# First expert's w2 in a row, guess's sums ahead of Newton's first step, two engines for the last stores, new step tables

## The chip, the cores and the metric

One core of a Trainium2 chip runs the whole kernel in one launch. The metric is device time in microseconds (us), from the first to the last work of the execution. Five engines take part, each working through a queue of its own in order: TensorE (PE, matmuls; PEld is its weight load), VectorE (DVE), ScalarE (ACT), GpSimd (POOL) and SyncE (SP, which issues most transfers).

## The reference

Nystrom attention over 8 batches x 8 heads, 576 tokens, head size 64, feeds a mixture of 8 experts (512 -> 1024 -> 512) in which a token either takes the expert of its own largest logit or keeps that of the token before.

```python
q_lm, k_lm = q.reshape(B,H,32,18,D).mean(3), k.reshape(B,H,32,18,D).mean(3)
A, Bm, C = sm(q, k_lm), sm(q_lm, k_lm), sm(q_lm, k)     # softmax of scaled products
Z = Bm.T / (norm1(Bm) * norminf(Bm) + 1e-6)
for _ in range(6): Z = 2 * Z - Z @ Bm @ Z               # Newton
x = A @ Z @ C @ v                                       # then [b, s, H * D]
logits = x @ w_gate
e = argmax(logits[b, s]) if s == 0 or sigmoid(x @ w_local) < 0.5 else prev_e
out[b, s] = softmax(logits)[e] * (relu(x[b, s] @ w1[e]) @ w2[e])
```

## The kernel before, in words

**Work.** For each batch the kernel computes A (32 landmarks by 576 tokens per head) and a small matrix W = Z C v, folds W into the expert's first weights (G = W w1, `w_w1`), and runs one expert over the batch's 576 tokens (`expert`): the expert that most of the batch's tokens take. Tokens of other experts are gathered later in slots of 128 (`slot_tokens` and so on; the sequence is batches 0 to 6, one slot, batch 7). Products that need full precision split an operand in a high and a low part, h and l: `split_w2` makes wh with a cast on ACT (line 720) and wl with a subtraction on POOL (line 725); `w_w1` makes gh on ACT (line 707) and gl on DVE (line 708).

**The expert.** A batch takes 16 chunks (`CH`): eight hidden tiles f for tokens 256 to 575 (first pass), then eight for tokens 0 to 255 (second pass). In a chunk `mm1` does six matmuls (line 737) into a PSUM bank, ACT and DVE make h, and two chunks later the second product (line 789, for a 64-token rest line 781) adds to the output banks. `store` scales the result and writes it out. The last stores of the kernel are those of blocks 0 and 1 of batch 7.

**Order.** All steps of the attention of the next batches are interleaved with the chunks by tables of times in chunks: `FIRST` (rest of batch 0), `SECOND` (batch 1), `PLANS` (batches 2 to 7), `W2_AT` (in which chunk of batch 0 the w2 tiles of batch 1 are loaded), `G_AT` (in which two chunks G of the next batch is made), `SLOT_AT`. A step with time t is emitted ahead of the half chunk that begins next. Up to the ninth chunk (`IN_ROW`) the PE's instructions are tied to the order of emission; the prologue ties PE, ACT, DVE and POOL. What is not tied, all of SP's issues among it, is ordered by the framework's scheduler by its own simulated times.

**The prologue** (`first_attention`, line 1009 on) works off batch 0 with nothing to overlap. There the first expert is guessed from the column sums of v: `guess_sums` (line 539, five matmuls for each of four head pairs, on PE), `guess_copy` (line 545, ACT), `guess_scores` (lines 551 and 554, PE and ACT), `guess` (lines 559 and 560, DVE). The index goes to a register of SP, and `first_weights` (line 1215) issues w1 in two pieces and one half, and w2 tiles of 256 KB each, four of which fit in the buffers `raw2` (`load_w2`, line 715; w1 by line 671). `keep_warm` (line 176) are matmuls without a use of their own. Newton's steps are line 432, the product C v is line 345. After the prologue `cuts_at` emits the split of tile 4 + i in chunk i.

**Gates of a batch.** `gates` (line 570) makes logits, `votes` (`eq`, line 584, then a matmul, line 588, and the index, line 593) picks the batch's expert, `get_w1` loads its weights. The room of v is one buffer (`v_t`, line 224): v of the next batch can only be loaded when C v of this one is done.

Of the kernel before, what the change touches and what calls it, by code (L numbers as in the profile page):

```python
# [9 lines left out]
F32 = mybir.dt.float32  # L10
# [10 lines left out]
P = 128  # L21
# [55 lines left out]
def nystrom_attn_then_sticky_moe(ctx, tc, qT, kT, v, wg, w12, out):  # L77
# [93 lines left out]
    def keep_warm(n, pz=None):  # L171


        pz = one.tile([P, 512]) if pz is None else pz
        for _ in range(n):
            nc.tensor.matmul(pz, zeros[:, 0:P], zeros[:, 0:pz.shape[1]], start=True, stop=True)
# [623 lines left out]
    def store(b, st, k, yp):  # L800
        ys = fk.tile([P, DM], F32, name="ys", bufs=2)
        t0 = b * S + k * P
        if b == B - 1 and k == 1:

            nc.scalar.mul(out=ys[:, 0:256], in_=yp[:, 0:256], mul=st["pw"][:, k:k + 1])
            nc.vector.tensor_scalar(out=ys[:, 256:512], in0=yp[:, 256:512], scalar1=st["pw"][:, k:k + 1], scalar2=None, op0=ALU.mult)
            nc.scalar.dma_start(out=out[t0:t0 + P, 0:256], in_=ys[:, 0:256])
            nc.sync.dma_start(out=out[t0:t0 + P, 256:512], in_=ys[:, 256:512])
        elif k < 4:
            nc.scalar.mul(out=ys, in_=yp, mul=st["pw"][:, k:k + 1])  # L810
            nc.scalar.dma_start(out=out[t0:t0 + P, :], in_=ys)
# [196 lines left out]
    def first_attention(st, st1):  # L1008
# [294 lines left out]
    PLANS = {
        2: (-13.4, -10.9, -9.4, -12.4, -7.9, -8.9, -7.9, -6.9, -5.9, -5.4, -5.9, -4.4, -1.9, -5.4, -1.9, -2.4, -0.9,
            -0.4, -0.9, -0.4, -0.4, 0.1, 2.1, -0.4, 3.6, 4.1, 5.1, 5.6, 6.6, 7.1, 8.1, 10.1, 8.1, 8.1, 8.6, 13.6,
            14.1),
        3: (-22.4, -16.9, -21.9, -15.9, None, -15.4, -13.4, -13.4, -13.4, -9.9, -8.9, -8.4, -6.4, -7.4, -2.9, -7.9,
            -8.4, -5.4, -6.9, -3.9, -2.9, -4.4, -3.9, -2.9, 1.1, 2.6, 2.6, 2.6, 3.1, 4.6, 3.6, 5.1, 8.1, 4.1, 7.6,
            10.1, 10.1),
        4: (-23.4, -17.9, -20.4, -16.9, None, -18.4, -15.9, -15.9, -15.4, -15.9, -14.4, -13.4, -11.4, -11.9, -10.4,  # L1310
            -9.4, -7.4, -7.4, -5.9, -8.4, -5.9, -6.4, -5.4, -7.4, -4.9, -5.4, -3.4, -2.9, 2.6, 3.1, 2.6, 3.1, 4.1,
            4.1, 4.1, 6.6, 10.1),
        5: (-26.4, -17.9, -24.4, -22.9, None, -16.9, -17.4, -16.9, -15.9, -16.4, -12.9, -14.9, -10.9, -11.4, -9.4,
            -11.9, -10.9, -10.4, -8.4, -10.4, -9.4, -9.4, -6.9, -3.9, -4.4, -1.9, -0.9, 1.6, 1.6, 2.1, 2.6, 4.6, 4.1,
            4.1, 4.1, 4.1, 6.1),
        6: (-21.9, -17.9, -20.9, -20.9, None, -17.4, -17.9, -16.9, -14.4, -14.4, -13.9, -13.9, -10.9, -12.4, -9.9,
            -12.4, -9.9, -9.9, -5.9, -8.4, -6.9, -8.9, -4.9, -4.9, -0.9, -3.4, -3.4, -2.4, 1.1, 2.1, 1.6, 4.6, 3.6,
            4.6, 4.6, 7.1, 7.6),
        7: (-26.9, -20.4, -25.4, -19.9, None, -20.9, -21.4, -17.9, -15.4, -15.9, -14.9, -13.9, -13.4, -14.4, -11.4,
            -12.9, -11.4, -11.4, -11.9, -10.4, -9.9, -10.9, -10.9, -7.9, -4.9, -7.4, -4.9, -4.9, -0.4, -4.4, -0.4,  # L1320
            1.1, 2.6, 3.1, 7.6, 7.6, 10.6),
    }
    G_AT = {0: (14, 15), 1: (14, 15), 2: (12, 15), 3: (14, 15), 4: (11, 14), 5: (13, 15), 6: (11, 15), 7: (2, 7)}
    SLOT_AT = (-11.5, -7.5, -7.0, -4.0, -3.5, 0.5, 1.0, 8.0, 7.6, -1.0, 25.0)
# [115 lines left out]
```

## Time and profile before

| | us |
|---|---|
| median of 3 runs | 483.35 (483.09 to 485.33) |
| the profiled execution | 482.71 |
| its span, first to last instruction | 480.9 |
| PE busy in the span | 457.2 (95%), 4709 matmuls |
| DVE, POOL, ACT busy | 275.3, 233.5, 205.0 |
| SP's queue of transfers | 66.83 MB, 39.9% of 16 DMA engines |

PE is busy nearly all the time, so what can be had lies in its idle stretches. Such a table is an average: which engine or transfer ends a wait is read stretch by stretch, from the views further down.

### The profile page before, as it was taken

Reading aid. Unit: us, or ns where it says so; the run is one execution under the profiler, and the core shown is the slowest. Engines: PE = TensorE matmul, PEld = TensorE weight load, DVE = VectorE, ACT = ScalarE, POOL = GpSimd, SP = SyncE. Lnnn points to the kernel's source line nnn. Section 1 sums busy time; section 2 is a strip of 40 time slices with the busy share of each in tenths; the row PEclk is TensorE's granted clock in tenths of the full one; section 3 lists DMA queues with packets and bytes.
Section 4 is the critical chain, followed back from the end, with each engine's and each line's share of the span. In section 5 each row is a group of like instructions: output and inputs, shape, how many; then the busy total and the mean of one; then the engine's idle time right before and its main releaser. Section 6 shows DMA issues by size and latency. Waiting matters only on the chain.

```text
span 480.9 us, 12154 instructions
## 1 busy us (share of the span) xinstructions
PE 457.2 (95%) x4709; PEld 338.7 (70%) x4709; DVE 275.3 (57%) x823; ACT 205.0 (43%) x519; POOL 233.5 (49%) x365
## 2 busy tenths in 40 slices
PE   8977799989999999999999999999999999999995
PEld 3544567567776687667886688767886787778884
DVE  6886876676578447837832584337647845333121
ACT  2445344463354724436342733346332614455131
POOL 7276655189057525654922463244335755277010
PEclk9989999999999999999999999999999999999998
DMA  8797055694069505965842316521621802672011
GB/s 299 260 373 268 0 210 198 235 355 153 8 215 397 183 7 198 350 206 201 290 137 93 133 48 266 176 72 51 258 106 46 315 7 52 211 262 82 0 57 46
DMA packets 38861, 82.01 MB, mean 171 GB/s; under 512 B 3291, under 2 KB 4827, under 8 KB 38032
## 3 DMA queue, kind: packets, MB, share of 16 engines
q1 hardware_dynamic: 32064, 66.83, 39.9%
q10 hardware_dynamic: 5248, 9.31, 5.5%
q0 software_dynamic: 1488, 5.07, 2.8%
q8 instruction: 38, 0.62, 0.5%
q14 instruction: 23, 0.19, 0.1%
HBM read 66.29 MB, written 14.94 MB: 169 GB/s over the span
## 4 chain that ended last, share of the span: by engine, by line
PE 71%; DMA 8%; DVE 8%; issue 5%; ACT 5%; POOL 2%; SPq 1%; ACTq 0%; POOLq 0%; DVEq 0%
PE py L789 32%; PE ph L737 19%; PE pg L781 6%; DMA raw<-w 5%; PE one L345 2%; PE one L432 2%; PE ph L694 2%; PE one L304 2%; DMA out<-ys 1%; PE one L331 1%; PE one L482 1%; DMA q_t<-qT 1%; POOL wl L725 1%; ACT ys L810 1%; DVE eq L584 1%
## 5 line engine op out<-in xcount | busy, mean ns | idle before, releaser
L789 PE MATMUL py<-wh,h 128*128 128x512 f32 x528 | 170.9, 402 | 1.7 <-DVE h L749 1.0
L725 POOL TENSOR_TENSOR wl<-raw,wh 128x512 fp32r<-128x512 f32 x72 | 92.2, 1296 | 75.1 <-ACT wh L720 55.4
L789 PEld LDWEIGHTS py<-wh,h 128*128 128x128 f32 x528 | 95.4, 188 | 29.5 <-issue 5.9
L746 ACT ACTIVATE h<-ph 128x256 fp32r<-128x256 f32 (+2 forms) x136 | 54.7, 403 | 129.5 <-PE ph L737 104.9
L749 DVE SCALAR_TENSOR_TENSOR h<-ph,h 128x256 fp32r<-128x256 f32 (+1 forms) x136 | 55.7, 410 | 89.7 <-ACT h L746 85.6
L789 PE MATMUL py<-wl,h 128*128 128x512 f32 x264 | 91.7, 394 | 0.0
L737 PE MATMUL ph<-ath,gh 128*128 128x320 f32 (+1 forms) x256 | 80.1, 313 | 1.7 <-DVE gl L708 1.7
L737 PE MATMUL ph<-ath,gl 128*128 128x320 f32 (+1 forms) x256 | 76.1, 297 | 0.0
L737 PE MATMUL ph<-atl,gh 128*128 128x320 f32 (+1 forms) x256 | 75.9, 296 | 0.0
L737 PEld LDWEIGHTS ph<-ath,gh 128*128 128x128 f32 x256 | 48.4, 189 | 15.4 <-issue 6.4
L789 PEld LDWEIGHTS py<-wl,h 128*128 128x128 f32 x264 | 49.4, 188 | 10.5 <-issue 0.8
L737 PEld LDWEIGHTS ph<-atl,gh 128*128 128x128 f32 x256 | 48.4, 189 | 3.7
L737 PEld LDWEIGHTS ph<-ath,gl 128*128 128x128 f32 x256 | 48.3, 189 | 1.0 <-issue 0.8
L720 ACT CAST wh<-raw 128x512 fp32r<-128x512 f32 x72 | 43.1, 629 | 12.7 <-DMA raw<-w 10.3
L810 ACT ACTIVATE ys<-py,pall 128x512 f32<-128x512 f32 x31 | 20.7, 691 | 12.4 <-PE py L789 5.1
L819 POOL TENSOR_TENSOR ys<-ys,yl 64x512 f32<-64x512 f32 x8 | 10.2, 1277 | 32.3 <-ACT yl L817 32.3
L494 POOL TENSOR_TENSOR sa<-sa,mxa 128x1152 f32<-128x1152 f32 x7 | 14.9, 2133 | 22.5 <-DVE mxa L493 22.5
L708 DVE TENSOR_TENSOR gl<-ph,gh 128x512 fp32r<-128x512 f32 (+1 forms) x19 | 12.4, 658 | 22.1 <-ACT gh L707 22.0
L707 ACT CAST gh<-ph 128x512 fp32r<-128x512 f32 (+1 forms) x19 | 10.6, 562 | 28.7 <-PE pg L694 26.8
L241 POOL TENSOR_TENSOR t<-q_t 128x288 f32<-128x288 f32 x28 | 20.4, 746 | 4.7 <-DMA q_t<-qT 1.7
L781 PE MATMUL pg<-wl,h 128*128 128x512 f32 x56 | 22.4, 400 | 0.0
L781 PE MATMUL pg<-wh,h 128*128 128x512 f32 x56 | 22.0, 394 | 0.0
(335 smaller groups left out, 730.8 us busy)
## 6 DMA issues: line engine op xcount, KB each, us to landing
raw<-w SPq DMA_DIRECT2D x72, 256.0 KB, 5.8
raw<-w SPq DMA_DIRECT2D x17, 1024.0 KB, 7.0
v_t<-v SPq DMA_DIRECT2D x8, 1024.0 KB, 8.0
out<-ys ACTq DMA_DIRECT2D x31, 256.0 KB, 3.0
q_t<-qT SPq DMA_DIRECT2D x6, 1152.0 KB, 5.4
k_t<-kT SPq DMA_DIRECT2D x6, 1152.0 KB, 9.2
ad<-sa POOLq DMA_DIRECT2D x8, 576.0 KB, 3.1
q_t<-qT SPq DMA_DIRECT2D x4, 576.0 KB, 7.8
```

Of the source, the lines that this page charges most:

```text
L241: nc.gpsimd.tensor_add(t9[:, i], src[:, a + i, :, 0:9], src[:, a + i, :, 9:18])
L494: nc.gpsimd.tensor_tensor(out=sa, in0=sa, in1=mx.unsqueeze(2).broadcast_to([P, 2 * NJ, M]), op=ALU.subtract)
L707: st["cut"] = nc.scalar.copy(out=gh[:, g, x], in_=ps[g][:, 0:n * P]).ins.name
L708: last = nc.vector.tensor_tensor(out=gl[:, g, x], in0=ps[g][:, 0:n * P], in1=gh[:, g, x].bitcast(F32), op=ALU.subtract)
L720: cut = nc.scalar.copy(out=wh, in_=raw)
L725: nc.gpsimd.tensor_tensor(out=wl, in0=raw, in1=wh.bitcast(F32), op=ALU.subtract)
L737: mm = nc.tensor.matmul(hp, w[:, g, c], x[:, g, s0:s0 + n], start=(i == 0), stop=(i == 5))
L746: nc.scalar.activation(out=h[:, 0:e], in_=hp[:, 0:e], func=AF.Relu)
L749: nc.vector.scalar_tensor_tensor(out=h[:, 384:384 + m], in0=hp[:, 0:m], scalar=0.0, in1=h[:, 0:m].bitcast(F32), op0=ALU.max, op1=ALU.subtract)
L781: nc.tensor.matmul(yps[4], hs[ff][1], w, start=(ff == 0 and w is w2[ff][0]), stop=(ff == NC2 - 1 and w is w2[ff][1]))
L789: nc.tensor.matmul(yps[full[i]], h[:, part + i * P:part + i * P + P], w, start=(f == 0 and part == 0 and w is wh), stop=(f == NC2 - 1 and ...
L810: nc.scalar.mul(out=ys, in_=yp, mul=st["pw"][:, k:k + 1])
```

## The change

- `first_weights`: all eight w2 tiles of the first expert are issued in a row. The last four go into a tile of v's room, `place`, instead of waiting for a `raw2` buffer; tiles 6 and 7 were loaded in chunks 0 and 1 before (`weights_at`). v of batch 1 is loaded at 4.1 chunks.
- `first_attention`: all sums of the guess stand ahead of Newton's first step, the scores behind it, the index behind the second. The `keep_warm` matmuls there are two in each of four places (4, 1, 1, 1 before).
- `store`: of the last batch, block 0 is scaled on DVE and stored by SP; block 1 is scaled half on ACT and half on DVE, into two tiles.
- New numbers in `SECOND`, `PLANS` (119 of 217 entries), `G_AT`, `SLOT_AT`, `FIRST` and `W2_AT`.

```diff
-    def load_w2(e, f):
+    def load_w2(e, f, raw=None):
-        raw = fw.tile([P, 512], F32, name="raw2", bufs=4)
+        raw = fw.tile([P, 512], F32, name="raw2", bufs=4) if raw is None else raw
...
-        if b == B - 1 and k == 1:
-
+        if b == B - 1 and k == 0:
+
+            nc.vector.tensor_scalar(out=ys, in0=yp, scalar1=st["pw"][:, k:k + 1], scalar2=None, op0=ALU.mult)
+            nc.sync.dma_start(out=out[t0:t0 + P, :], in_=ys)
+        elif b == B - 1 and k == 1:
+
+            yr = fk.tile([P, 256], F32, name="yl", bufs=1)
             nc.scalar.mul(out=ys[:, 0:256], in_=yp[:, 0:256], mul=st["pw"][:, k:k + 1])
-            nc.vector.tensor_scalar(out=ys[:, 256:512], in0=yp[:, 256:512], scalar1=st["pw"][:, k:k + 1], scalar2=None, op0=ALU.mult)
+            nc.vector.tensor_scalar(out=yr, in0=yp[:, 256:512], scalar1=st["pw"][:, k:k + 1], scalar2=None, op0=ALU.mult)
             nc.scalar.dma_start(out=out[t0:t0 + P, 0:256], in_=ys[:, 0:256])
-            nc.sync.dma_start(out=out[t0:t0 + P, 256:512], in_=ys[:, 256:512])
+            nc.sync.dma_start(out=out[t0:t0 + P, 256:512], in_=yr)
...
+        SUMS = (2, 2, 2, 2)
...
-        keep_warm(4, first_bank[:, 128:512])
+        keep_warm(SUMS[0], first_bank[:, 128:512])
         done(n)
         done(f)
         c_max(1, 0)
         a_turn(0, 1)
+        guess_sums(st, range(NPAIR))
+        guess_copy(st)
         newton_step(0, st, 0)
         idle = psa.tile([P, 512], F32, name="one")
-        keep_warm(1, idle)
-        guess_sums(st, (0, 1))
+        keep_warm(SUMS[1], idle)
+        guess_scores(st)
         c_max(1, 1)
         c_exp(1)
         newton_step(0, st, 1)
-        guess_sums(st, (2, 3))
-        guess_copy(st)
+        guess(st)
+        keep_warm(SUMS[2], idle)
         a_turn(1, 1)
         newton_step(0, st, 2)
-        keep_warm(1, idle)
-        guess_scores(st)
+        keep_warm(SUMS[3], idle)
         a_max0(0, 1)
-        guess(st)
-        keep_warm(1, idle)
         newton_step(0, st, 3)
         first_weights(st)
...
-        load_v(1, sts[1])
-        for f in range(4, 6):
-            get_w2(0, f)
+        place = ld.tile([P, NBLK, DM], F32, name="v_t", bufs=1)
+        for f in range(4, NC2):
+            raws[0, f] = load_w2(e, f, place[:, f - 4, :])
...
-        if i < 2:
+        if i < 2 and b:
             get_w2(b, NC2 - 2 + i)
...
-    SECOND = dict(q0=0.1, k0=0.1, c0=0.6, q2=2.1, k2=2.6, c1=3.1, norms=3.1, a0=6.1, nf=6.6, a1=7.1, t0=7.1, amax=8.1,
-        n0=7.6, t2=7.6, n1=8.1, t4=8.1, aexp=8.1, n2=7.6, cv=8.1, n3=7.6, n4=8.1, anorm=8.1, n5=8.1, nw=8.1, gw=8.6,
-        aback=8.6, gates=9.1, nwt=11.6, votes=9.1, split=10.6, w1=9.6, w1b=11.7, fresh=12.6, sticky=14.6, chosen=15.6,
-        own=16.6)
+    SECOND = dict(v=4.1, q0=0.1, k0=0.1, c0=0.6, q2=0.6, k2=1.1, c1=2.6, norms=2.6, a0=6.1, nf=7.1, a1=7.1, t0=7.1,
+        amax=8.1, n0=7.6, t2=7.6, n1=7.6, t4=7.6, aexp=8.1, n2=7.6, cv=8.1, n3=7.6, n4=8.1, anorm=8.1, n5=8.1, nw=8.1,
+        gw=8.1, aback=8.6, gates=8.6, nwt=11.1, votes=8.6, split=8.6, w1=9.1, w1b=11.2, fresh=11.6, sticky=12.1,
+        chosen=14.6, own=17.6)
...
-    G_AT = {0: (14, 15), 1: (14, 15), 2: (12, 15), 3: (14, 15), 4: (11, 14), 5: (13, 15), 6: (11, 15), 7: (2, 7)}
+    G_AT = {0: (14, 15), 1: (14, 15), 2: (13, 15), 3: (14, 15), 4: (11, 14), 5: (13, 15), 6: (13, 14), 7: (2, 7)}
...
-    FIRST = dict(rs=0.1, rm=0.1, re=0.1, rn=0.1, rb=2.6, gw=1.6, gates=3.1, votes=3.1, fresh=4.6, sticky=5.6,
-        chosen=6.1, own=9.1)
-    W2_AT = (11, 11, 12, 12, 15, 15)
+    FIRST = dict(rs=0.6, rm=0.6, re=0.6, rn=1.1, rb=2.1, gw=3.1, gates=3.6, votes=5.6, fresh=6.1, sticky=6.1,
+        chosen=6.1, own=7.1)
+    W2_AT = (11, 12, 12, 12, 12, 15)
```

## Rows read from the trace of the kernel before

**Rows 1.** Busy time by stretch: us, busy us of each engine (instructions), PE clock, DMA share, GB/s

```profile
24.00:60.00 36.00, 27.85 (x237) 17.54 (x237) 28.06 (x80) 16.11 (x53) 23.74 (x34) 0.95 0.59 214
60.00:100.00 40.00, 36.38 (x508) 24.95 (x507) 26.88 (x78) 16.87 (x47) 19.02 (x30) 1.00 0.63 225
100.00:450.00 350.00, 346.10 (x3486) 263.93 (x3485) 197.51 (x600) 156.40 (x376) 178.15 (x244) 1.00 0.47 164
450.00:476.00 26.00, 24.94 (x136) 21.31 (x134) 4.42 (x12) 7.05 (x16) 1.27 (x1) 1.00 0.09 27
```

**Rows 2.** Waits of PE, 24 to 62 us: us in total, times, longest

```profile
PE py L694 <- DMA raw<-w: 2.1, 1, 2.1
PE pg L781 <- DVE bt L390: 1.7, 1, 1.7
PE ph L737 <- DVE gl L708: 1.4, 1, 1.4
```

**Rows 3.** Waits of PE, 84 to 100 us

```profile
PE ph L694 <- DMA raw<-w: 2.3, 2, 1.7
```

**Rows 4.** Timeline of SP's issues: start, us, what [idle before, releaser]

```profile
19.97 1.18 SPq L671 DMA_DIRECT2D raw<-w  x2
...
23.00 1.26 SPq L715 DMA_DIRECT2D raw<-w  x2
...
30.45 0.34 SPq L715 DMA_DIRECT2D raw<-w  x1
...
87.06 0.39 SPq L671 DMA_DIRECT2D raw<-w  x1
88.18 0.95 SPq L715 DMA_DIRECT2D raw<-w  x2
89.33 0.38 SPq L671 DMA_DIRECT2D raw<-w  x1
```

**Rows 5.** Timeline of ACT around 37 us

```profile
37.33 0.62 ACT L720 CAST wh<-raw 128x512 fp32r<-128x512 f32 x1 [3.13 <-DMA raw<-w]
...
38.02 0.57 ACT L707 CAST gh<-ph 128x512 fp32r<-128x512 f32 x1
```

**Rows 6.** The instructions of line 584: ns min/median/max, first and last start

```profile
L584 DVE TENSOR_TENSOR eq<-lg,mxl x8: 190/269/3548, 47.4 to 378.2; 128x40 bf16<-128x40 f32 x8
```

**Rows 7.** Timeline of POOL around 50 us

```profile
49.64 1.28 POOL L725 TENSOR_TENSOR wl<-raw,wh 128x512 fp32r<-128x512 f32 x1
```

**Rows 8.** Timeline of the guess on PE, ACT and DVE, 14 to 20 us

```profile
14.32 0.81 PE L176 MATMUL one<-zeros 128*128 128x384 bf16 x4
...
16.11 0.64 PE L539 MATMUL one<-ones,v_t 128*128 128x1 bf16 x10
...
18.21 0.35 PE L551 MATMUL one<-wg_sb,vs 128*128 128x8 bf16 x8
...
17.96 0.16 ACT L545 CAST vs<-one 128x4 bf16<-128x4 f32 x1
...
19.07 0.16 DVE L560 FIND_INDEX8 regs<-top,tot 128x8 uint32<-128x8 f32 x1
```

**Rows 9.** Busy time by stretch, 27 to 30 us, columns as in rows 1

```profile
27.00:30.00 3.00, 3.00 (x22) 1.30 (x7) 2.02 (x5) 1.68 (x4) 0.86 (x1) 0.50 1.05 386
```

**Rows 10.** Timeline of the end, 475 to 481 us

```profile
475.31 0.69 ACT L810 ACTIVATE ys<-py,pall 128x512 f32<-128x512 f32 x1 [2.57 <-PE py L789]
...
476.39 0.48 DVE L806 TENSOR_SCALAR ys<-py,pall 128x256 f32<-128x256 f32 x1 [3.20 <-ACT ys L805]
...
476.90 0.35 SPq L808 DMA_DIRECT2D out<-ys  x1
```

**Rows 11.** Chain that ended last, a chunk of a second pass: start, us, what

```profile
159.53 1.39 PE py L789 x6
160.91 0.89 PE ph L737 x6
```

**Rows 12.** DMA issues of v: count, KB each, median us to landing

```profile
v_t<-v SPq DMA_DIRECT2D x8, 1024.0 KB, 8.0
```

More of the change, by code (lines that the diff above doesn't have):

```diff
@@ L1303, in nystrom_attn_then_sticky_moe @@
     PLANS = {
-        2: (-13.4, -10.9, -9.4, -12.4, -7.9, -8.9, -7.9, -6.9, -5.9, -5.4, -5.9, -4.4, -1.9, -5.4, -1.9, -2.4, -0.9,
-            -0.4, -0.9, -0.4, -0.4, 0.1, 2.1, -0.4, 3.6, 4.1, 5.1, 5.6, 6.6, 7.1, 8.1, 10.1, 8.1, 8.1, 8.6, 13.6,
+        2: (-13.4, -11.4, -9.9, -12.4, -7.9, -9.4, -7.9, -7.4, -6.9, -6.4, -6.9, -4.9, -2.4, -5.4, -1.4, -1.4, 0.1,
+            -0.4, -0.9, -0.4, -0.4, 1.1, 2.6, -0.9, 4.6, 4.6, 5.1, 5.6, 7.1, 7.1, 8.1, 10.1, 8.1, 8.1, 8.6, 13.6,
             14.1),
-        3: (-22.4, -16.9, -21.9, -15.9, None, -15.4, -13.4, -13.4, -13.4, -9.9, -8.9, -8.4, -6.4, -7.4, -2.9, -7.9,
-            -8.4, -5.4, -6.9, -3.9, -2.9, -4.4, -3.9, -2.9, 1.1, 2.6, 2.6, 2.6, 3.1, 4.6, 3.6, 5.1, 8.1, 4.1, 7.6,
-            10.1, 10.1),
@@ L1310, in nystrom_attn_then_sticky_moe @@
[L1310 to L1321, printed above, removed]
-    }
@@ L1323, in nystrom_attn_then_sticky_moe @@
-    G_AT = {0: (14, 15), 1: (14, 15), 2: (12, 15), 3: (14, 15), 4: (11, 14), 5: (13, 15), 6: (11, 15), 7: (2, 7)}
-    SLOT_AT = (-11.5, -7.5, -7.0, -4.0, -3.5, 0.5, 1.0, 8.0, 7.6, -1.0, 25.0)
+        3: (-22.4, -16.9, -19.4, -13.9, None, -15.4, -13.4, -13.4, -13.4, -9.9, -8.4, -8.4, -6.4, -6.9, -2.9, -7.9,
+            -8.4, -6.4, -7.9, -4.4, -2.9, -3.9, -3.4, -2.4, 1.1, 2.6, 2.6, 2.6, 3.1, 5.1, 4.1, 4.1, 7.6, 5.1, 7.1,
+            11.1, 11.6),
+        4: (-24.4, -20.9, -18.4, -17.4, None, -16.4, -15.4, -15.4, -14.9, -14.9, -14.9, -13.4, -11.4, -11.9, -10.9,
+            -8.9, -7.4, -7.4, -6.4, -8.4, -6.4, -6.4, -6.4, -7.4, -5.9, -5.4, -3.9, -3.9, 2.6, 4.1, 2.6, 2.6, 3.6,
+            4.1, 5.1, 6.6, 11.6),
@@ new lines, in nystrom_attn_then_sticky_moe @@
+        5: (-26.9, -20.4, -25.4, -24.4, None, -16.9, -18.4, -16.9, -16.9, -16.4, -12.9, -14.9, -10.9, -11.4, -10.4,
+            -11.9, -10.9, -10.4, -7.9, -11.4, -7.9, -9.9, -7.9, -4.4, -3.9, -1.9, -1.4, 0.6, 1.1, 4.1, 2.6, 5.6, 3.6,
+            3.6, 4.1, 4.1, 6.6),
+        6: (-21.4, -17.9, -20.9, -20.4, None, -17.4, -17.9, -16.9, -13.9, -14.9, -13.9, -14.4, -11.4, -13.4, -9.9,
+            -12.4, -9.9, -9.9, -5.9, -8.4, -6.9, -9.4, -5.4, -4.9, -0.9, -3.4, -2.9, -2.4, 0.6, 2.6, 1.6, 3.6, 3.1,
+            3.1, 3.6, 6.6, 7.6),
@@ L1325, in nystrom_attn_then_sticky_moe @@
+        7: (-27.4, -20.4, -25.9, -19.4, None, -20.4, -20.4, -17.4, -14.9, -16.4, -14.9, -13.9, -13.4, -14.4, -11.9,
+            -12.9, -11.4, -10.9, -11.9, -10.4, -9.9, -10.4, -10.4, -9.4, -5.4, -6.9, -5.9, -5.4, -0.4, -3.9, -0.4,
+            1.1, 1.6, 3.6, 7.6, 7.6, 10.1),
+    }
+    G_AT = {0: (14, 15), 1: (14, 15), 2: (13, 15), 3: (14, 15), 4: (11, 14), 5: (13, 15), 6: (13, 14), 7: (2, 7)}
+    SLOT_AT = (-13.5, -4.5, -8.0, -4.0, -2.0, 0.5, 1.5, 9.0, 8.6, -0.5, 26.5)
     TURN = 6
-    FIRST = dict(rs=0.1, rm=0.1, re=0.1, rn=0.1, rb=2.6, gw=1.6, gates=3.1, votes=3.1, fresh=4.6, sticky=5.6,
-        chosen=6.1, own=9.1)
```

## The prediction

> **What bounds the kernel now.** I read first the busy time by stretch [rows 1]: in 100 to 450 us TensorE (PE) works 346.10 of 350.00 us, so there is little to gain there. From 24 to 60 us it works 27.85 of 36.00 and from 60 to 100 us 36.38 of 40.00: 8.15 and 3.62 us of idleness, in the stretch where the first expert runs and nothing has been prepared ahead. VectorE (DVE) is busy 28.06 us in the first of them, more than PE; keep that in mind. Second I read what PE waited for [rows 2, 3]. The largest waits from 24 to 62 us are 2.1 us for the second piece of w1 (a transfer), 1.7 us behind DVE, 1.4 us for G's second cut gl; the rest of the 8.15 is small pieces. From 84 to 100 us all of it is one cause: 2.3 us for the second expert's w1. Third, the queues that explain those waits. SyncE (SP) issues the first expert's w1 at 19.97, but its fifth w2 tile only at 30.45, because there are four raw2 buffers and it needs the first one back, and the last three follow one by one [rows 4]. ScalarE (ACT) stood 3.13 us for that fifth tile, and the cut gh of G, at 38.02, was queued behind it [rows 5]: that is the 1.4 us. DVE's `eq` took 3548 ns where the median of its eight is 269 [rows 6], and the 1.7 us is behind it: it ended at 50.98, when the split of w2 on GpSimd (POOL) from 49.64 was over [rows 7]. Last, the end: three rows from 475.31 to 476.90 [rows 10].
>
> **The sum is made** against the profiled execution's own time, 482.71 us (span 480.9, the rest lies around it). The median shown, 483.35, is 0.64 above; I add that at the end. A measurement of this kernel can tell about 0.5%, 2.4 us, from no change.
>
> **1. The guess, 0.7 us.** The twenty sums of v (L539), ten in 0.64 us, move ahead of Newton's first step, and the filler ahead of them falls from four matmuls (0.81 us from 14.32) to two [rows 8]. Sums then run from about 14.7 to 16.0. ACT is not yet in the second exponentials that now delay the copy to 17.96 [rows 8]. Behind the copy come Newton's step (about 0.4), two fillers (0.4), the scores (0.35), another copy (0.16): 17.4. The index needs DVE, behind the next Newton add, and I put its end at 18.5 instead of 19.07 + 0.16 = 19.23 [rows 8]. So SP loads w1 0.7 us earlier; bounds 0.3 (DVE's queue as long as now) and 1.2 (nothing queued). Newton's chain itself slips by about 0.5 us, since 1.3 us of sums now fill a gap that was shorter. That costs nothing, because PE then waits 2.1 us for w1's second piece anyway [rows 2]; without that cover it would cost the 0.5. The second exponentials on ACT wait for the scores' copy by about as much, under the same cover. The fillers are seven before and eight after, the other new ones stand where PE waits for DVE.
>
> **2. w2 in a row, 3.3 us.** The tiles 4 to 7 go into the room of v of batch 0. Its readers are the guess's sums and the product C v, done before SP gets there (after two w1 pieces, w1's second half and four w2 tiles, near 24 us), so the new wait should be met on arrival. From 27 to 30 us the transfers run at 386 GB/s with the DMA engines full [rows 9], so a 256 KB tile takes 0.68 us. The fourth tile left at the end of the pair at 23.00 to 24.26 [rows 4]; the fifth follows it now instead of leaving at 30.45. It leaves some 6 us sooner, and with four tiles now in a row I expect it some 4 us ahead of the 37.3 at which the cut of [rows 5] could start; the other three follow it. ACT's 3.13 us and PE's 1.4 us go whole. Of the 8.15 us there then remain 2.1 for w1, which stay, and 4.65 in small waits. The 1.7 us hang on `eq`, which the new table moves from 3.1 to 5.6, when the splits are over: I take 1.0 of them. Of the other 2.95, which follow ACT's lateness through the rest of batch 0's scores and the gates, I take a third, 0.9, because DVE has its own queue there. Together 1.4 + 1.0 + 0.9 = 3.3; bounds 0 (all of it turns into waits for DVE) and 6.05 (all but w1). Not below 0 for the transfers, as nothing is put ahead of w1.
>
> What moves with it: v of batch 1 leaves the full stretch and is issued at 4.1 chunks. SP then waits there for the cut and the last split of tile 7; behind it stand batch 3's loads and batch 1's own weights, both wanted later still. Batch 1 uses v at 8.1 chunks, four chunks on. A chunk is at least 2.28 us [rows 11] and has many small steps beside it here, so there are more than 9 us for a transfer that takes 8.0 [rows 12]: costed at nothing. If this cover went, PE would wait for the product with v as it does for w1 in [rows 3], some 2 us.
>
> Here a page speaks. The row is `eq`: 3548 ns, beside splits on POOL of 1.28 us each, against 269 [rows 6, 7]. The Trainium skill, "SBUF — State Buffer", section "Who interferes with whom", says that a DVE instruction with two SBUF inputs and a GpSimd instruction that reads SBUF exclude one another, the second waiting until the first is finished. By that `eq` would gain one split's time, 1.28 us of the 3.3, and in the same share the sum would hold 0.4 where it holds 1.0. The trace agrees that the two exclude one another, but its wait is longer than one split. What speaks against this change is that the earlier splits now meet other two-input work of DVE; that is the first rival below.
>
> **3. The second expert's w1, 1.8 us.** Gates, votes and the w1 load of batch 1 move half a chunk ahead. A chunk of the second pass is six matmuls L789 and six L737, 1.39 + 0.89 us [rows 11], so half is 1.14. And W2_AT puts one w2 tile less between the halves of w1; now there are two, the pair at 88.18 between 87.06 and 89.33 [rows 4]: 0.68 us. Together 1.8 of the 2.3 us wait [rows 3]; bounds 0 (the votes' matmul keeps its place in PE's queue and the halves meet other traffic) and 2.3. The displaced w2 tiles come later, but G's cuts stand ahead of theirs on ACT.
>
> **4. The end, 0.3 us.** Block 0 goes to DVE and SP, block 1 to ACT and DVE into separate tiles. Now DVE's half starts at 476.39, released by ACT's half of the same tile, and its store at 476.90 is the last [rows 10]. After: DVE takes block 0 from 475.31. Its 256 columns cost 0.48, so 512 lie between 0.48 and 0.96; I take 0.75, an estimate nearer to the 0.69 that ACT needs for the same tile. Then its half of block 1 ends at 476.54, and SP, done with block 0's store, issues at 476.56: 0.34 sooner, and I take 0.3; bounds 0.1 and 0.45.
>
> **5. The tables of batches 2 to 7, 0.** 119 of 217 entries move, nearly all by 0.5 or 1.0 chunk, both ways. The cover is the 3.90 us of idleness in 350 us [rows 1]: gain at most some 1.5, and as much to lose if a step lands ahead of its operands.
>
> Sum: 0.7 + 3.3 + 1.8 + 0.3 = 6.1. 482.71 - 6.1 = 476.6, and with the 0.64 to the median **477.2 us**.
>
> **The rivals.** First, DVE becomes the bound: it has 28.06 us of work where PE would now need 30 [rows 1]. For it: `eq` shows how long one small instruction can take beside POOL, and the earlier splits move that to other work. Against: DVE is relieved of 3.3 us by the same step. Then only the guess, the end and 0.7 us of part 3 remain, 1.7: 481.0 in its own time, 481.6. Chance 0.17.
>
> Second, slower: in batches 2 to 7 steps placed earlier stand in PE's queue ahead of their operands, and PE, working in order, waits. Place: the steps q0 to n5 that moved. Price: a wait like the 1.7 us of [rows 2] once a batch, 6 x 1.7 = 10.2, giving 487.4. It decides from 6.1 / 6 = 1.0 us a batch. For it: that is how PE waits behind DVE at 54 us. Against: in the 350 us all waits together are 3.90 now, with tables of the same kind. Chance 0.11.
>
> Third, the change does not do what it says: SP's order is not among the pinned ones, and if the tiles 4 to 7 are placed behind the loads of batch 2 or are held by v's room, part 2 is lost and 0.7 + 1.8 + 0.3 = 2.8 are left: 480.5. Chance 0.08.
>
> **How the numbers follow.** The forecast has the other 0.64. Within it the bounds of part 2 are the widest; in the good direction 2.7 more from there, 0.5 each from parts 1 and 3, and some of the clock: the granted clock stood at 0.50, the lower level of 1.2 GHz, from 27 us on, after the wait for w1 [rows 9], and three us at half speed are 1.5 us of work. Not all at once, so the low end is 473.0. The high end is 482.0, which takes in the first and third rivals and leaves out the second and some of the edges. Faster by over 0.5% (under 480.9): nearly all of the forecast, a third of the first rival, half of the third: 0.73. Slower (over 485.8): most of the second: 0.08. The rest is 0.19.
>
> **What would show it.** Right: the first w1 issue near 19.2; the eighth w2 issue of batch 0 before 27; no wait of ACT for raw after 34; `eq` under 1 us; PE idle from 24 to 60 under 5.5 us; the wait for the second w1 under 1 us; the last store issued within 1.2 us of the last matmul. Wrong: PE idle in 24 to 60 us unchanged with DVE as releaser, or over 6 us of idleness in 100 to 450 us.

## The result, and the profile after

| | before | after |
|---|---|---|
| median, us | 483.62 (483.09 to 485.33, 4 runs) | 476.38 (475.99 to 477.26, 4 runs) |
| ratio, 95% interval | | 0.9847 (0.9818 to 0.9876) |
| the profiled execution, us | 482.71 | 476.7 |
| its span, us | 480.9 | 474.9 |

7.2 us were gained against the 6.1 of the sum: the median was forecast as 477.2 and came to 476.38, the profiled execution was to take 476.6 and took 476.7. A second profile of the same kernel (after_again below) took 477.8, so a match to 0.1 us is luck. Whether the sum is right for its own reasons is another question, and most of this section's rows and all of the experiments go to it.

First the busy time by stretch, after (columns: us, busy us of each engine with its instructions, granted clock, DMA share, GB/s). It answers to [rows 1].

```profile
24.00:60.00 36.00, 31.37 (x285) 20.02 (x284) 28.36 (x88) 17.55 (x57) 24.64 (x38) 0.95 0.58 203
60.00:100.00 40.00, 38.71 (x529) 27.55 (x528) 27.62 (x80) 20.56 (x51) 22.13 (x29) 1.00 0.75 276
100.00:450.00 350.00, 346.28 (x3452) 264.03 (x3453) 190.43 (x593) 152.19 (x368) 172.53 (x240) 1.00 0.46 158
```

PE's idle time fell from 8.15 to 4.63 us in the first stretch (3.5), from 3.62 to 1.29 in the second (2.3), and from 3.90 to 3.72 in the third (0.2). That is 6.0 us, which is also by how much the span is shorter; the end takes 0.3 of it back, and PE's busy time up to its last matmul is some 0.4 less in this record than in the one before, which was not followed up. The second profile of the change is idle for 5.29 us from 24 to 60, so these tenths hold for one execution. Now who is waited for, after: PE's waits from 20 to 62 us, and below the dots the longest from 62 to 110 us (us in total, times, longest), which answer to [rows 2, 3]:

```profile
PE one L274 <- ACT ql L247: 2.6, 1, 2.6
PE ph L737 <- DVE atl L530: 0.4, 1, 0.4
...
PE py L694 <- DMA raw<-w: 0.3, 1, 0.3
...
PE one L432 <- DVE et L435: 0.5, 1, 0.5
```

The three waits of [rows 2] are gone or small (2.1 for w1's second piece is 0.3 now), the 2.3 for the second expert's w1 is gone. In their place stands one that was not there: 2.6 us for `ql`. ACT's timeline, after, tells why (start, us, what, idle before it and its releaser).

```profile
30.85 1.29 ACT L720 CAST wh<-raw 128x512 fp32r<-128x512 f32 x2 [2.68 <-DMA raw<-w]
32.05 0.38 ACT L746 ACTIVATE h<-ph 128x256 fp32r<-128x256 f32 x1
...
32.43 0.26 ACT L247 ACTIVATE ql<-sq 128x64 f32<-128x64 f32 x1
...
36.71 0.59 ACT L707 CAST gh<-ph 128x512 fp32r<-128x512 f32 x1 [0.27 <-PE pg L694]
```

ACT stands 2.68 us in front of the third w2 tile's cut; behind it in ACT's queue are the first chunk's h and the landmark `ql` of batch 1, and for `ql` PE waits. In the kernel before, `ql` stood ahead of that cut, which began at 32.22 after waiting 0.61 us:

```profile
31.35 0.26 ACT L247 ACTIVATE ql<-sq 128x64 f32<-128x64 f32 x1
```

So two things came together: the first chunk begins 2.5 us earlier (its first matmul at 26.64 instead of 29.11) while the third tile's cut can begin only 1.4 us earlier (30.85 instead of 32.22), and on ACT that cut now stands first. The cut of [rows 5], which waited 3.13 us, waits no more, and `gh` comes at 36.71 instead of 38.02. What the third tile waits for is the transfers: first SP's timeline of issues, after, then the busy time by stretch from 24 to 36 us.

```profile
18.93 0.99 SPq L671 DMA_DIRECT2D raw<-w  x2
...
22.68 0.88 SPq L715 DMA_DIRECT2D raw<-w  x2
23.83 2.08 SPq L715 DMA_DIRECT2D v_t<-w  x4
...
81.76 0.39 SPq L671 DMA_DIRECT2D raw<-w  x1
82.36 0.39 SPq L715 DMA_DIRECT2D raw<-w  x1
83.40 0.38 SPq L671 DMA_DIRECT2D raw<-w  x1
```

```profile
24.00:28.00 4.00, 3.11 (x40) 1.26 (x39) 3.28 (x9) 2.79 (x7) 2.53 (x5) 1.00 1.04 356
28.00:32.00 4.00, 2.17 (x26) 1.30 (x24) 3.97 (x6) 1.26 (x3) 2.71 (x3) 1.00 1.08 393
32.00:36.00 4.00, 3.26 (x32) 0.93 (x32) 2.56 (x9) 2.40 (x10) 4.00 (x5) 0.59 1.00 403
```

All eight w2 tiles have left by 25.91, and from 24 to 36 us the DMA engines are full (share 1.00 and more, 356 to 403 GB/s). After the idle time from 30 to 33 us the granted clock of 32 to 36 us is 0.59; before, it had fallen at 27 us [rows 9]. The fall has moved and not gone. In the second half of the listing w1 of the second expert leaves at 81.76, 5.3 us before the 87.06 of [rows 4].

The timeline of the end, after, to be set beside [rows 10]:

```profile
468.56 0.61 PE L789 MATMUL py<-wh,h 128*128 128x512 f32 x2
469.05 0.75 DVE L805 TENSOR_SCALAR ys<-py,pall 128x512 f32<-128x512 f32 x1 [2.18 <-PE py L789]
469.21 0.47 ACT L810 ACTIVATE ys<-py,pall 128x256 f32<-128x256 f32 x1 [2.80 <-PE py L789]
469.72 0.36 ACTq L812 DMA_DIRECT2D out<-ys  x1
...
469.82 0.35 SPq L806 DMA_DIRECT2D out<-ys  x1
470.28 0.37 SPq L813 DMA_DIRECT2D out<-yl  x1
```

The last store is issued 1.11 us after the last matmul's end (469.17), against 1.41 before; but the span ends 5.73 us after that matmul, against 5.41.

### The profile page after: what moved, and what is told of

Same layout as the page of the kernel before. It is cut to its first block, busy times and chain, and to the rows that moved or that the text cites. A ratio compares the mean times of both kernels' runs of the same rounds, so it can differ in the third digit from the quotient of the medians.

```text
span 474.9 us, 12149 instructions
## 1 busy us (share of the span) xinstructions
PE 456.8 (96%) x4710; PEld 338.1 (71%) x4710; DVE 268.7 (57%) x824; ACT 204.6 (43%) x518; POOL 231.5 (49%) x365
## 4 chain that ended last, share of the span: by engine, by line
PE 76%; DVE 7%; DMA 6%; issue 4%; ACT 3%; POOL 2%; SPq 1%; ACTq 0%; POOLq 0%; DVEq 0%
PE py L789 33%; PE ph L737 20%; PE pg L781 5%; DMA raw<-w 3%; PE ph L694 3%; PE one L432 2%; PE one L345 2%; DMA k_t<-kT 2%; PE one L482 2%; PE one L331 2%; DMA q_t<-qT 1%; PE one L304 1%; PE one L274 1%; DVE h L749 1%; POOL t L241 1%
## 5 line engine op out<-in xcount | busy, mean ns | idle before, releaser
L725 POOL TENSOR_TENSOR wl<-raw,wh 128x512 fp32r<-128x512 f32 x68 | 86.9, 1294 | 73.2 <-ACT wh L720 65.0
L720 ACT CAST wh<-raw 128x512 fp32r<-128x512 f32 x68 | 41.0, 631 | 15.7 <-DMA raw<-w 13.9
L241 POOL TENSOR_TENSOR t<-q_t 128x288 f32<-128x288 f32 x28 | 21.4, 785 | 4.3 <-DVE sk L242 1.7
```

Source lines behind the costliest of these rows:

```text
L241: nc.gpsimd.tensor_add(t9[:, i], src[:, a + i, :, 0:9], src[:, a + i, :, 9:18])
L720: cut = nc.scalar.copy(out=wh, in_=raw)
L725: nc.gpsimd.tensor_tensor(out=wl, in0=raw, in1=wh.bitcast(F32), op=ALU.subtract)
```

## The experiments

Each ran beside the kernel before on the same chip; ratios are to the kernel before.

| run | what | median | ratio (95%) |
|---|---|---|---|
| after_again | the change | 475.5 | 0.9856 (0.9824 to 0.9887) |
| a1_guess_only | guess alone | 483.55 | 0.9996 (0.9974 to 1.0017) |
| a2_w2_only | w2's row alone | 481.75 | 0.9974 (0.9947 to 1.0001) |
| a5_no_guess | change less guess | 477.01 | 0.9852 (0.9823 to 0.9881) |
| a6_no_w2_row | change less w2's row | 482.07 | 0.9953 (0.9925 to 0.9982) |
| a7_old_w1 | change less batch 1's dates of w1 | 483.41 | 0.9979 (0.9955 to 1.0002) |
| a4_old_plans | change less tables of 2 to 7 | 479.37 | 0.9919 (0.9887 to 0.9951) |
| b1_old_first_second | change less tables of 0 and 1 | 488.35 | 1.0116 (1.0080 to 1.0153) |
| a3_old_end | change less the end | 476.12 | 0.9869 (0.9839 to 0.9899) |
| b2_cuts_late | change, w2's cuts later | 483.17 | 1.0006 (0.9977 to 1.0035) |
| b5_two_cuts | the same, nearer to the change | 476.26 | 0.9849 (0.9818 to 0.9881) |
| b3_block0_first | change, last sums by block | 474.43 | 0.9842 (0.9808 to 0.9877) |

**after_again.** 

> The changed kernel itself once more, on the chip and beside the runs that the three variants of this call share, so that they can be set against it: 476.4 us, ratio 0.985 (0.982 to 0.988), if the first comparison holds. The kernel with the old tables of batches 2 to 7 came to 0.9919; if this run comes to 0.988 or less, the new tables do carry time, against the prediction's 0 for them; at 0.990 or more they don't.

The first comparison holds, and with it a4's difference from the change. Below, what a part is worth within the change is its run's ratio less 0.985, the middle of the two comparisons, times 483; since each interval is some 0.003 to either side, such a difference is good to about 2 us.

### Each of two parts alone

**a1_guess_only**: the kernel before with the prologue's new order.

```diff
+        guess_sums(st, range(NPAIR))
+        guess_copy(st)
         newton_step(0, st, 0)
...
-        guess_sums(st, (0, 1))
+        guess_scores(st)
```

> The kernel before with the guess's new order alone. Theory (the parts add up, each through the transfers): the first w1 issue comes near 18.9 us instead of 19.97 and the first chunk about 1 to 2.5 us earlier, but the fifth w2 tile still waits for a raw2 buffer and ACT still stands for it over 2.5 us, so of the time only 0.7 to 1.0 us is gained: 482.6 to 482.9. Rival (the transfers are saturated and everything behind is ordered by the last w2 tile): no gain, 483.6. Second rival (the guess alone is what brought the 2.5 us at the first chunk, and it is kept): 481.1.

w1 left at 18.91 instead of 19.97, and PE's wait for its second piece fell from 2.1 to 0.55 us. Yet the time is the same, within 1 us. The profile is of the longest of a1's twelve runs (486.51; the median is 483.55), so its waits may be larger than usual. The longest wait of PE from 24 to 62 us in a1:

```profile
PE one L274 <- ACT ql L247: 5.3, 1, 5.3
```

and in ACT's timeline of a1 what stood ahead of that `ql`:

```profile
33.41 0.62 ACT L720 CAST wh<-raw 128x512 fp32r<-128x512 f32 x1 [5.26 <-DMA raw<-w]
```

This is the third tile, issued at 23.12 into a free buffer and cut ten microseconds later: it waits for its transfer, as in the change, and not for room. PE reached the work behind `ql` earlier (the first chunk began at 26.62 instead of 29.11) and waited there. A gain ahead of a queue that is set by transfers was handed back at that queue.

**a2_w2_only**: the kernel before with the row of eight and v of batch 1 at 4.1; all other dates as before.

```diff
+        place = ld.tile([P, NBLK, DM], F32, name="v_t", bufs=1)
+        for f in range(4, NC2):
+            raws[0, f] = load_w2(e, f, place[:, f - 4, :])
```

> The kernel before with the eight w2 tiles in a row alone, and v of batch 1 at 4.1 chunks; guess, end and tables as before. Theory: ACT no longer waits 3.13 us for the fifth tile in front of G's cut, PE's 1.4 us goes, and eq (still at 3.1 chunks) takes under 1 us because the splits on POOL are over by then; PE idle from 24 to 60 us falls from 8.15 to 5 to 6 us, the time by 2 to 3: 480.6 to 481.6. Rival (the wait only moves: ACT stands for tiles 2 and 3 ahead of the hidden tile and the landmarks): idle stays over 7, time 483.

Some 1.2 us, an interval that just reaches no change. By busy time PE is idle 5.46 us from 24 to 60 us (30.54 busy of 36), 2.7 less than before, and 2.55 from 60 to 100, 1.1 less; of these 3.8 us the profiled run's span keeps 2.5 and the median 1.2. A part of the difference is the clock: the granted clock of a2 is 0.93 from 0 to 24 us and 0.91 from 24 to 60, before it was 1.00 and 0.95. And a2's twelve times run from 479.5 to 483.7, so the profiled one (480.15) lies below the median. What a2 does settle is `eq`: the instructions of line 584 (ns minimum, median and maximum) in a2, where a1 still has a maximum of 3545:

```profile
L584 DVE TENSOR_TENSOR eq<-lg,mxl x8: 186/270/1011, 48.2 to 376.3; 128x40 bf16<-128x40 f32 x8
```

With `votes` at the old 3.1 chunks the long `eq` is gone as soon as the splits are done early: the first takes 0.57 us, and the maximum of 1011 is batch 6's, which takes 1012 in the kernel before too. So the row frees it without the new date. The reverse holds as well: in a6 below, without the row and with the new date, the first `eq` takes 0.19 us. Either is enough.

### Parts taken out of the change

**a5_no_guess**: the change with the old order of the prologue (the diff of a1, backwards). 

> The changed kernel with the old order of the guess's sums, so that w1 is issued near 20.0 again instead of 18.9. Alone on the kernel before, the new order brought nothing (0.9996), since ACT then waited 5.3 us for w2 and PE with it. Theory: with w2 in a row the transfers follow w1 directly, so the guess is worth what w1 comes earlier: 1.0 us, of which the fall of the clock may add some: 477.0 to 478.0. Rival: the 2.6 us for w2's third tile is the bound at the front whichever way w1 comes, and it is no more than 0.3 us slower than the changed kernel.

The rival, as far as the times can tell (0.9852 against 0.985, good to 2 us). In its profile w1 leaves 0.44 us ahead of A's exponentials on ACT (line 1098) where in the change it leaves 1.60 ahead, and PE waits 0.9 instead of 0.3 us for its second piece. Then, in PE's waits from 20 to 62 us of a5,

```profile
PE one L274 <- ACT k_t L249: 2.6, 1, 2.6
```

and in its busy time by stretch:

```profile
24.00:60.00 36.00, 31.28 (x284) 20.27 (x287) 28.28 (x86) 17.61 (x58) 24.49 (x38) 0.95 0.60 213
```

The same 2.6 us, behind the same cut, this time with `k_t` queued behind it; idle from 24 to 60 us 4.72, as against 4.63. The guess brings nothing that can be seen, alone or within the change. Why not within it, the start of the first chunk shows. Counted from the second `ql` of batch 0 on ACT (L247, near 10 us), its first matmul comes after 19.07 us in the kernel before, 16.49 in a1, 16.64 in a5 and 16.49 in the change. The guess alone starts the first chunk 2.6 us earlier, and so nearly do the other parts without it: the two gains are the same gain.

**a6_no_w2_row**: the change with the loads of w2 and of v as before. 

> The changed kernel with w2 loaded as before: four rooms, tiles 5 to 8 one by one, v of batch 1 in their midst. All else, the new tables too, stays. Theory: the prediction's step of 3.3 us, and the wait of 5.3 us on ACT that the guess alone brought, return: 480 to 483, ACT waiting 3 us or more for raw before G's cut. Rival: as the row alone on the kernel before brought only 1.2 us (0.9974), it is worth about that here: 477.5 to 478.

The theory: about 5 us, good to 2, and ACT waits as named, first for the third tile (2.68 us in the change) and then for the fifth, by its timeline in a6:

```profile
32.63 0.62 ACT L720 CAST wh<-raw 128x512 fp32r<-128x512 f32 x1 [3.96 <-DMA raw<-w]
...
37.98 0.62 ACT L720 CAST wh<-raw 128x512 fp32r<-128x512 f32 x1 [2.67 <-DMA raw<-w]
```

PE is idle for 7.57 us from 24 to 60 us (28.43 busy), close to the 8.15 before.

**a7_old_w1**: the change with the dates of batch 1 around its weights, and `W2_AT`, as before.

```diff
-        gw=8.1, aback=8.6, gates=8.6, nwt=11.1, votes=8.6, split=8.6, w1=9.1, w1b=11.2, fresh=11.6, sticky=12.1,
+        gw=8.6, aback=8.6, gates=9.1, nwt=11.6, votes=9.1, split=10.6, w1=9.6, w1b=11.7, fresh=11.6, sticky=12.1,
...
-    W2_AT = (11, 12, 12, 12, 12, 15)
+    W2_AT = (11, 11, 12, 12, 15, 15)
```

> The changed kernel with the second batch's gates, votes and both w1 loads, and the dates of its w2, as before. Theory: PE's wait for the second expert's w1 near 84 to 92 us returns with 1.5 to 2.3 us, and the time is 478 to 479. Rival: w1 is early anyway now, since the first expert is done 2.5 to 4 us earlier while its transfers are no longer held up, and nothing over 0.5 us returns: 476 to 477.

The wait came back as the theory had it, but neither time came: the cost is some three times as large, about 6 us by the times and 4.7 by the span of the profile. PE's longest wait from 62 to 110 us in a7:

```profile
PE ph L694 <- DMA raw<-w: 1.8, 2, 1.5
```

and two rows of PE's timeline later on, waits that the change has in part (0.4 for `mx`) or not:

```profile
153.35 0.61 PE L694 MATMUL ph<-raw,wt 64*32 64x512 f32 x1 [1.13 <-DVE gl L708]
161.67 0.39 PE L737 MATMUL ph<-ath,gh 128*128 128x320 f32 x1 [1.10 <-DVE mx L311]
```

PE lost 1.1 us from 60 to 100 and 2.0 from 100 to 200 (96.39 against 98.44 busy). Of the rest no single wait can be named.

**a4_old_plans**: the change with `PLANS`, `G_AT` and `SLOT_AT` as before. 

> The changed kernel with the old tables of batches 2 to 7 (PLANS, G_AT, SLOT_AT). Theory: they carry nothing that can be measured, PE idle from 100 to 450 us within 0.5 us of 3.72, time 476.4 within 0.8. Rival (they carry a part of the gain): 1.5 us or more slower, 477.9 and up.

The rival: about 3.3 us are lost, and PE is idle for 5.92 us from 100 to 450 us, not 3.72. Up to 150 us no stretch differs from the change by more than 0.8 us; then, in PE's timeline of a4 and in its busy time by stretch:

```profile
159.56 0.39 PE L737 MATMUL ph<-ath,gh 128*128 128x320 f32 x1 [2.22 <-DVE mx L311]
```

```profile
155.00:160.00 5.00, 2.78 (x30) 2.07 (x29) 2.81 (x12) 2.13 (x5) 3.61 (x4) 1.00 0.71 205
...
162.00:164.00 2.00, 2.00 (x7) 1.62 (x6) 1.17 (x6) 2.00 (x9) 0.12 (x1) 0.50 0.06 19
```

PE, in order, stands 2.2 us for a step of the softmax (`mx`, DVE), and behind it the granted clock drops to 0.50, the level of 1.2 GHz. In the change this wait is 0.4 us. So the second rival's mechanism is real, and it strikes when the old dates meet the new front, not when the new ones do.

**b1_old_first_second**: the change with `FIRST`, `SECOND` (all but v) and `W2_AT` as before. 

> The changed kernel with the old tables of batches 0 and 1 (FIRST, SECOND except v, W2_AT). Theory: the wait for the second expert's w1 comes back at 1.5 to 2.5 us and some small waits, time 476.4 + 2 to 3 = 478.4 to 479.4; eq at 3.1 chunks stays under 1 us, since it was the early splits and not the table that freed it. Rival (the table freed eq): eq over 3 us again and 1.7 us more on PE, 480.5.

Slower than the kernel before, by 1.2%, so both forecasts missed, though `eq` was short, as the theory had it (0.18 us for the first). It has the row, the guess, the end and the new later tables, and its first stretch is nearly as good as in the change (5.24 us idle against 4.63 and 5.29 in the change's two profiles); what it loses lies from 60 to 100 us, by the busy time of b1 by stretch and PE's longest wait from 60 to 100 us:

```profile
24.00:60.00 36.00, 30.76 (x279) 18.90 (x267) 27.28 (x88) 16.93 (x57) 24.59 (x37) 0.95 0.54 195
60.00:100.00 40.00, 33.66 (x444) 22.32 (x442) 22.63 (x68) 15.05 (x42) 16.90 (x24) 0.96 0.58 203
```

```profile
PE one L451 <- DVE et L435: 2.8, 1, 2.8
```

PE reaches the product that makes batch 1's W (L451) ahead of its operand from DVE, and stands. The wait for the second expert's w1 is back too, 2.4 us from 60 to 110.

### The new wait for ql

**b2_cuts_late**: the cuts of tiles 2 and 3 go behind ACT's work that PE waits for, tiles 4 to 7 follow later.

```diff
-        if i < 5:
+        if i < 5 and b:
...
-        if b == 0 and i < 4:
-            cut_w2(b, NC2 - 4 + i)
+        if b == 0:
+            for f in {2: (4, 5), 3: (6,), 4: (7,)}.get(i, ()):
+                cut_w2(b, f)
...
+        for mark in late:
+            not_ahead_of(cut, mark)
```

> The changed kernel with the cuts of w2's tiles 2 and 3 put behind ACT's first landmarks of the second batch and ACT's part of the second chunk, and those of tiles 4 to 7 one to two chunks later. In the changed kernel ACT stands 2.7 us at the cut of tile 2 for its DMA, and PE 2.6 us for the landmark queued behind it, after which the granted clock falls to 0.50 for some 3.5 us. Theory: that wait is order on ACT alone, so it goes, and with it the fall of the clock: 2 to 4 us less than the changed kernel, 472.5 to 474.5. Rival: the second half of w1 or the chunks on DVE are late next at the same place, PE waits 1.5 us or more between 27 and 36 us for another reason, and the time is within 1 us of the changed kernel.

Both missed. The wait went and the clock kept 1.00 from 24 to 36 us, as the theory had it, but 5.4 us came back at one place: PE's longest wait from 24 to 62 us in b2, and in POOL's timeline the rows on which it hangs:

```profile
PE one L570 <- DVE at L1116: 5.4, 1, 5.4
```

```profile
43.49 1.42 POOL L241 TENSOR_TENSOR t<-q_t 128x288 f32<-128x288 f32 x2
44.88 1.05 POOL L1111 TENSOR_TENSOR sa<-sa,rsa 128x512 f32<-128x512 f32 x1
```

The gates (L570) need the normalised scores; their last product on POOL came at 44.88 instead of 42.78, behind the last split and two squares of batch 1. The span is 5.7 us longer than the change's; from 24 to 60 us PE is idle for 2.8 of them (7.40 against 4.63), and for 2.6 more up to 200 us, which were not followed up.

**b5_two_cuts**: as b2, with `{2: (4, 5), 3: (6, 7)}`. 

> As b2_cuts_late, but with the cuts of tiles 4 to 7 all at chunks 2 and 3, one chunk earlier for two of them. In b2 the wait of 2.6 us before the landmark was gone and the clock kept at 1.00 from 24 to 36 us, and PE then lost 5.4 us near 48 us, behind DVE's transposes at the end of batch 0's gate chain: on GpSimd that chain's last product came only at 44.88, behind the last split and two squares of batch 1, against 42.78 in the changed kernel. Here GpSimd has it behind four splits and the square of k alone, as in the changed kernel. Theory: the 5.4 us were that place in GpSimd's queue, so they go to under 2 us, and the gain at the front stays: PE idle from 24 to 60 us under 4 us (4.6 changed kernel, 7.4 in b2), time 472.5 to 475. Rival: the end of the gate chain is set by the transfers of batch 1's k and by DVE, not by that place; then PE still waits 4 us or more near 46 to 49 us and the time is 478 to 483.

Between the two. The place in POOL's queue was worth 3 of the 5.4 us, and the time is that of the change. The timeline of b5 at the gates, and its busy time by stretch:

```profile
41.89 1.05 POOL L1111 TENSOR_TENSOR sa<-sa,rsa 128x512 f32<-128x512 f32 x1
42.98 0.77 DVE L1116 STREAM_TRANSPOSE at<-sa 128x256 f32<-128x256 f32 x2
43.57 1.28 PE L570 MATMUL one<-at,wgc 128*32 128x160 f32 x16 [2.29 <-DVE at L1116]
```

```profile
42.00:48.00 6.00, 4.43 (x28) 3.71 (x29) 5.53 (x20) 1.57 (x6) 5.13 (x8) 0.72 0.75 281
```

The 2.6 us at `ql` are now 2.3 us at the gates, with the fall of the clock behind them (0.72 from 42 to 48 us; in the change 1.00 there). Idle from 24 to 60 us is 4.68, as against 4.63 in the change and 4.72 in a5. Three orders of the front give the same idle time, within what profiles of one front differ by (4.4 to 5.6 in the change, after_again, a3, a4, a7 and b3). In b5 what is won at the transfers is waited off at the gates, whose chain runs through DVE and POOL. A later date for the gates in b5, which would let PE do a chunk first, was not tried.

### The end

**a3_old_end**: the change with the old last stores. 

> The changed kernel with the end of the kernel before. In the profile of the changed kernel the last store was issued 1.11 us after the last matmul (1.41 before) but the span ended 5.73 us after it (5.41 before). Theory: the last 512 KB end when they have been moved, not when they have been issued, so the two engines bring nothing: within 0.3 us of the changed kernel. Rival (the prediction's term): the earlier issue carries through, and this kernel is 0.3 us slower (0.1 to 0.45). The times of whole runs can hardly tell 0.3 us; the stretch from the last matmul to the end of the span can: 5.7 by the theory, 6.0 by the rival.

From the last matmul to the end of the span: 5.39 us (467.61 to 473.0) with the old end, where 5.7 or 6.0 was expected. The other three profiles with the old end (before, a1, a2) have 5.3 to 5.4, and all ten with the new one have 5.7. The old end is the shorter by 0.3, which whole runs can't tell (0.9869 against 0.9856). Its issues in the timeline of a3, after the last matmul at 467.61, and the busy time of a3 by half microseconds:

```profile
468.15 0.34 ACTq L811 DMA_DIRECT2D out<-ys  x1
...
469.03 0.35 SPq L808 DMA_DIRECT2D out<-ys  x1
```

```profile
468.60:469.10 0.50, 0.00 (x0) 0.00 (x0) 0.40 (x1) 0.00 (x0) 0.00 (x0) 1.00 0.21 78
469.10:469.60 0.50, 0.00 (x0) 0.00 (x0) 0.00 (x0) 0.00 (x0) 0.00 (x0) 1.00 1.05 385
```

The first store is issued 0.54 us after the last matmul in the old end (468.15) and 0.55 in the new one (469.72 less 469.17), and about 1 us later the DMA engines are full (385 GB/s in the second of these rows). An earlier second and third issue has nothing to fill. The Trainium skill, "DMA: Bandwidth & Descriptors", section "Issuing engines are not separate DMA queues", says just that: stores issued by several engines run on the same DMA engines, and only the issue time is saved. The traces agree: 0.30 us of issue saved, none of it at the end. Why the new end is 0.3 us longer, and not equal, stays open; the moving itself ends later, for from 3.00 to 3.25 us after the last matmul the change's DMA share is still 0.19 and that of a3 is 0.

**b3_block0_first**: the last eight matmuls in the order of output blocks. 

> The changed kernel with the last eight matmuls of w2 put in the order of output blocks instead of chunks, so that the first block's sum ends some 0.6 to 0.7 us earlier before the last matmul than now and its 256 KB start that much earlier. Theory (the end is bound by the moving of the last 512 KB): the stretch from the last matmul to the end of the span falls from 5.7 to 5.0 to 5.3 us, the whole to 475.9. Rival (it is bound by the issue and latency of the very last store): 5.7 as now, no change.

No change that can be told (5.68 us; 0.9842 against 0.9856), but it doesn't test the theory: by the trace, block 0's sum did not end earlier. Block by block the last six matmuls would read wh, wl, wh, wh, wl, wh; in b3 as in the change they read wh, wl, wh, wl, wh, wh, and in both DVE takes up block 0 some 0.1 us after the end of the last but one (468.29 and 468.20; in the change 469.05 and 468.95). PE is not tied to the order of emission there, so the earlier store never happened.

## Why the prediction was right, and where it was not

**The places** are right: 3.5 us of idle time from 24 to 60 us, where 0.7 + 3.3 were forecast; 2.3 from 60 to 100, where 1.8 were; 0.2 in the rest, where 0 was. The signs named ahead came out, too: w1 at 18.93 (near 19.2), the eighth w2 issue before 25.91 (27), no wait of ACT for raw after 34 us, the first `eq` 0.28 us, no wait for the second w1, the last store 1.11 us after the last matmul. The third rival is out by the same rows: the eight tiles do go in a row. What failed are shares of the sum.

**1. The guess, 0.7: nothing seen, alone or within the change.** The times alone, good to 1 and 2 us, don't exclude 0.7. The index came at 18.03 rather than 18.5 and w1 1.0 us earlier, more than I took. The step that failed is "so SP loads w1 0.7 us earlier" taken as a gain in time: in a1 the next wait, for w2's third tile, takes it back, and a5 shows that within the change the first chunk starts only 0.15 us later without the new order.

**2. w2's row, 3.3: 1.2 alone, about 5 (good to 2) within the change.** Gone whole are ACT's 3.13 us, the 1.4 for gl and the 1.7 behind `eq`, of which I took 1.0, by `eq`'s new date; a2 shows that the row frees `eq` at the old date, and a6 that the date does it without the row. Missing from the sum is the wait that took their place, 2.57 us for `ql`. I had followed the tiles 5 to 8 and not asked when the third lands, with the DMA engines full and a queue in order on ACT behind its cut. It does not come from the row: a1 and a6, which lack the row, have it with 5.3 and 4.0 us. That v of batch 1 costs nothing is borne out: the longest wait from 62 to 110 us is 0.5.

By the rule on `eq` the sum would have held 0.4 of the 1.7 where I put 1.0. The Trainium skill, "SBUF — State Buffer", section "Who interferes with whom", has the waiting instruction go on when the other is finished. Here, from POOL's timeline, is what POOL did in the kernel before while `eq` took 3.55 us, from 47.43 to 50.98:

```profile
47.95 0.25 POOL L599 TENSOR_SCALAR fr<-lg 128x5 f32<-128x5 f32 x1
48.18 1.28 POOL L725 TENSOR_TENSOR wl<-raw,wh 128x512 fp32r<-128x512 f32 x1
49.42 0.25 POOL L609 TENSOR_TENSOR pe<-lg,mxl 128x40 f32<-128x40 f32 x1
```

Another split had been under way since 46.69, and the split of [rows 7] follows right behind. POOL's instructions stood end to end, and `eq` got through only at the end of that split, two whole splits after the one under way when it began. This wait doesn't agree with a wait of one instruction. Others do: batch 6's `eq` in the change began within a split that ended at 324.40, and was through at 324.46, though POOL went straight on at 324.36.

```profile
323.11 1.29 POOL L725 TENSOR_TENSOR wl<-raw,wh 128x512 fp32r<-128x512 f32 x1
323.44 1.02 DVE L584 TENSOR_TENSOR eq<-lg,mxl 128x40 bf16<-128x40 f32 x1
```

A row of POOL instructions without a gap is thus not enough to hold `eq` for several of them; what was different at 47.43 is not shown. With the splits done early, the first `eq` took 0.28 us.

**3. The second expert's w1, 1.8: the 2.3 of the wait, and some 6 us (good to 2) if it is taken out.** The wait itself was sized well (a7 brings back 1.8). For the other 4 the reading is that a late second expert upsets batches whose dates were set for an early one; a7's waits near 153 and 161 us fit it, but it is not shown.

**4. The end, 0.3: measured -0.3 in the profiles, nothing in the times.** The step that failed is "SP issues ... 0.34 sooner, and I take 0.3", which took the last issue for the end. That the first issue and the moving of 512 KB set the end fits the rows of a3 and is not shown, since b3 did not test it.

**5. The tables of batches 2 to 7, 0: right for the stretch (3.90 and 3.72 us idle), wrong as a price.** Leaving them as they were costs 3.3 us (a4).

So 0.3 was too much and 0.7 isn't seen, 0 for the late tables and 1.8 were too little by what their removal costs, and the sum came out all the same, in part by luck. The single removals add up to 14.5 us (5.0 + 6.2 + 3.3, each good to 2) where the change brings 7.2, and the two parts that were run alone bring about 1.4 together: the terms are not independent, so a sum of them can't be shown right. Of the rivals, the first (DVE is the bound, 481.6) did not happen as a whole, but b5 shows its place: past the transfers the gates' chain on DVE and POOL is next. The second (PE in order ahead of its operands, 487.4) is what b1 and a4 show, with the old tables.

## What to carry to other kernels

Take each part out of the finished change as well as putting it alone into the old kernel: here the two parts put in alone gave about 1.4 us and three taken out 14.5, and only both together show that the parts need each other. Where two parts bring the same gain, as the first chunk's earlier start here, taking out one shows nothing. Dates set by hand belong to one front; whoever shortens the front sets the later dates anew, or PE arrives ahead of its operands, and behind the longer waits the clock falls (behind 2.57 and 2.22 us here; behind the 1.4 and 1.7 us of [rows 2] it stayed at 1.00). A wait that goes is worth only the distance to the next one on the same path: list what is late next (here the third tile, then the gates) before giving it its full price.

## What the runs showed of the hardware

- `eq`, 40 elements per partition, took 3.55 us beside a row of POOL instructions end to end, past two whole splits; beside other such rows it waited only for the one instruction under way (1.02 us at 323.44 in the change).
- Behind PE's wait of 2.57 us in the change and that of 2.22 in a4 the granted clock stood at 0.50, its lower level of 1.2 GHz, from 33 to 35 and from 162 to 164 us. In the kernel before it stood there at 27 us, behind the wait for w1, and in b5 it fell behind the gates: the loss moves with the wait.
- 512 KB of last stores end no sooner when the later ones are issued 0.3 us sooner.
